# A fused GELU layer with its backward pass: two loads moved from SyncE's queue to GpSimd's, and one transposing load cut in two

## The chip, the cores and the metric

The kernel runs on one core of a Trainium2 chip. The metric is the device time of one execution in microseconds. Before the change it is 267.49 us, the median of three runs (266.95, 267.49 and 268.2). A profile adds one more execution, whose trace is what the prediction is read from.

Engines are called TensorE (PE in the profile), VectorE (DVE), ScalarE (ACT), GpSimd (POOL) and SyncE (SP). SP computes nothing here; it issues DMAs, and so do ScalarE and GpSimd.

## The reference

Everything is in bfloat16: x and grad_out are 2048 x 448, w1 is 448 x 1792, w2 is 1792 x 448. The six outputs are the layer's result and the gradients of its five inputs:

```python
def _fwd_reference(x, w1, b1, w2, b2):
    h = jnp.einsum("bsd,df->bsf", x, w1) + b1
    h = _gelu(h)                      # tanh form
    return jnp.einsum("bsf,fd->bsd", h, w2) + b2
# outputs: out, and from jax.vjp with grad_out: grad x, w1, b1, w2, b2
```

With u = x w1 + b1, q = g w2^T and gh = q * gelu'(u), the work is five big products: u, q, out = gelu(u) w2, grad x = gh w1^T, and the two weight gradients x^T gh and h^T g.

## The kernel before, in words

**Two stages.** The first, up to about 177 us, goes over the rows in 4 blocks of 512 and over the 1792 features in 7 pairs of 128-wide tiles. Each step has one pair of one block: u of a pair (transposed: features on partitions), its GELU and derivative on ScalarE and VectorE, q of a pair, gh, and shares of out and grad x. The second stage makes the weight gradients.

**Order of the first stage.** The order is written out by hand. Iteration i of the loop (i = 1 to 11) makes u of step i + 2 (tile pu, from w1_f and xT), then q of step i (pq, from w2T and gT), with products for out (ps, from hT and w2_sb) and, from iteration 6 on, for grad x (ps, from ghT and w1T_sb) between them. Nearly all of these matmuls are recorded at line 259, in half_product, which runs two half-height products side by side. The feature pairs of a block are taken in the order FP = [1, 2, 3, 4, 5, 6, 0], so tiles 0 and 1 of each weight come last. Up to step 11 there is one accumulator for q (two banks): q of step i can begin only when gh of step i - 1 has been made from it, at line 397 on VectorE.

**Where the loaded tiles are first read.** x's second block by u of step 7, in iteration 5. w2_sb's tiles 0 and 1 by out's last pair, at the end of iteration 5. b2_bc (b2 on all partitions) when the first finished out tiles are evicted by VectorE at line 437, in iteration 6. w1T_sb's tiles 2 to 7 at the end of iteration 6; its tiles 8 and 9 as the first fill of iteration 7, tiles 10 and 11 as the second, tiles 12, 13, 0 and 1 after these. g's second block by q of step 7, in iteration 7, behind the second fill.

**The loads.** All loads are issued at the top, in the order of the code on each engine's queue. SP has most of them: plain ones (load_w1, load_w2, load_rest) and transposing ones (load_x, load_g, load_w2T, and the two w1T_sb parts). Two transposing loads are never issued from different engines. GpSimd has b1 (line 143), the last rows of w1 for tiles 0 and 1 (line 175, by load_rest at line 123), held back behind one of SP's loads by behind(), and a small copy into w2T (line 176). After that GpSimd issues the stores of finished tiles of out and grad x (line 438) and a few more loads. The DMAs of SP and ScalarE use eight semaphores in turn, so that each issue waits for the landing of the one eight issues earlier; GpSimd's use eight others in the same way.

The end of SP's list, with the line numbers of the profile:

```python
    load_w2T(1280, F)                                                  # 170
    load_x(1)                                                          # 171
    load_w2(nc.sync, 0, 2)                                             # 172
    nc.sync.dma_start(out=b2_bc[:], in_=b2....to_broadcast((P, D)))    # 173
    behind(nc.gpsimd, rest)                                            # 174
    load_rest(nc.gpsimd, 0, 256)                                       # 175
    nc.gpsimd.tensor_copy(out=w2T[DL:P, 0, 0:16], in_=w2_first[...])   # 176
    load_w2T(0, 256)                                                   # 177
    nc.sync.dma_start_transpose(out=w1T_sb[:, 0:8, :], ...)            # 178
    load_g(1)                                                          # 179
    nc.sync.dma_start_transpose(out=w1T_sb[:, 8:NF, :], ...)           # 180
```

SP's next instructions are the turn of gh for the second stage (line 409, in turn_gh), further blocks of x and g, and the stores of h (line 406).

Of the kernel before, what the change touches and what calls it, by code (L numbers as in the profile page):

```python
# [19 lines left out]
def kernel(  # L20
# [15 lines left out]
    nc = tc.nc  # L36
    P = 128
    B, S, D = x.shape
    F = w1.shape[1]
    assert (B, S, D, F) == (1, 2048, 448, 1792)  # L40
    NS = S // P
    NF = F // P
# [34 lines left out]
    b2_bc = const.tile([P, D], BF16, name="b2_bc")  # L77
# [5 lines left out]
    w1T_sb = const.tile([P, NF, D], BF16, name="w1T_sb")  # L83
# [12 lines left out]
    def wide(src, r0, n, shift):  # L96
        return bass.AP(src.tensor, src.offset + r0 * D - shift, [[D, n], [1, (KF + 1) * P]])

    def load_x(b):
        t = blk.tile([P, KF + 1, SB], BF16, name="xT", tag="xT")  # L100
        r0 = ROW0[b]
        if b in WIDE:
            nc.sync.dma_start_transpose(out=t[:], in_=wide(x2, r0, SB, 0))
        else:
            nc.sync.dma_start_transpose(out=t[:, 0:KF, :], in_=x2[r0:r0 + SB, 0:KF * P])
            nc.sync.dma_start_transpose(out=t[:, KF, :], in_=x2[r0:r0 + SB, D - P:D])
        xT[b] = t

    def load_g(b):
        t = blk.tile([P, KF + 1, SB], BF16, name="gT", tag="gT")  # L110
        r0 = ROW0[b]
        if b in WIDE:
            nc.sync.dma_start_transpose(out=t[:], in_=wide(g2, r0, SB, DL))
        else:
            nc.sync.dma_start_transpose(out=t[:, 1:KF + 1, :], in_=g2[r0:r0 + SB, DL:D])
            nc.sync.dma_start_transpose(out=t[:, 0, :], in_=g2[r0:r0 + SB, 0:P])
        gT[b] = t
# [4 lines left out]
    def load_rest(eng, f0, f1):  # L122
        return eng.dma_start(out=wt1[0:DL, f0:f1], in_=w1[KF * P:D, f0:f1])

    def behind(eng, transfer):
        tc.add_manual_dep(eng.nop().ins, transfer.ins.name, mybir.DependencyInfo(mybir.DependencyClass.Sync, mybir.DependencyReason.DATA),
                          reason="loads behind what is needed first")

    def load_w2(eng, t0, t1):
        return eng.dma_start(out=w2_sb[:, t0:t1, :], in_=w2[t0 * P:t1 * P, :].rearrange("(ft p) d -> p ft d", p=P))  # L130

    def load_w2T(f0, f1):
        if f0 > 0:
            nc.sync.dma_start_transpose(out=w2T[:, :, f0:f1], in_=wide(w2, f0, f1 - f0, DL))
        else:
            nc.sync.dma_start_transpose(out=w2T[:, :, 16:f1], in_=wide(w2, 16, f1 - 16, DL))
            nc.sync.dma_start_transpose(out=w2T[:, 1:KF + 1, 0:16], in_=w2[0:16, DL:D])
# [31 lines left out]
    load_w1(nc.sync, 0, 256)  # L169
    load_w2T(1280, F)  # L170
    load_x(1)
    load_w2(nc.sync, 0, 2)
    nc.sync.dma_start(out=b2_bc[:], in_=b2.rearrange("(o d) -> o d", o=1).to_broadcast((P, D)))
    behind(nc.gpsimd, rest)
    load_rest(nc.gpsimd, 0, 256)
    nc.gpsimd.tensor_copy(out=w2T[DL:P, 0, 0:16], in_=w2_first[0:DL, :])
    load_w2T(0, 256)
    nc.sync.dma_start_transpose(out=w1T_sb[:, 0:8, :], in_=w1[:, 0:8 * P])
    load_g(1)
    nc.sync.dma_start_transpose(out=w1T_sb[:, 8:NF, :], in_=w1[:, 8 * P:F])  # L180

    pw = two_banks(1, "pw")
    for w in range(NWAKE):
# [675 lines left out]
```

## Time and profile before

| | before |
|---|---|
| median of 3 runs | 267.49 us (266.95 to 268.2) |
| profiled execution | 266.88 us |
| its span, first to last instruction | 265.1 us |
| granted TensorE clock | 1.00 of full speed throughout |
| longest share of the chain that ended last | PE, 97% |

The span is 1.78 us shorter than the execution's own time; those are what lies before the first and after the last instruction. In the profile a row of a timeline gives start, duration, engine, line, operation, what is written and what is read. SPq and POOL rows named DMA are the issuing of a transfer, not the transfer; its landing is in the DMA view, counted from the start of the issue. In the list of waits the numbers are microseconds in total, how often, and the longest.

### The profile page before, as it was taken

The numbers are of one execution on the slowest core, as the hardware profiler recorded it, in microseconds if no ns is written. First come the engines' busy times: TensorE is split into PE (matmuls) and PEld (weight loads), VectorE is DVE, ScalarE is ACT, GpSimd is POOL, SyncE is SP. The second block draws the span as 40 slices with busy tenths as digits, with TensorE's granted clock in tenths as the row PEclk, the third lists the DMA queues.
The fourth block names the chain that finished last, engine by engine and source line by source line (L and its number), as shares of the span: only waits on it lengthen the run. The fifth ranks groups of instructions, "written<-read, shape, count | busy, mean of one in ns | idle before, by whom it ended". The sixth has DMA issues, their size and how long they took to land.

```text
span 265.1 us, 5205 instructions
## 1 busy us (share of the span) xinstructions
PE 261.2 (99%) x2171; PEld 148.2 (56%) x2171; DVE 174.8 (66%) x217; ACT 137.5 (52%) x164; POOL 41.4 (16%) x52
## 2 busy tenths in 40 slices
PE   8999999999999999999999999999999999999995
PEld 3444444444466565555657887764444765555554
DVE  1699999999998978769897631129999991000000
ACT  2899997888997596877748410022111111121111
POOL 1001003300302021010311110220700008900000
PEclk9999999999999999999999999999999999999999
DMA  7999999999999999255382359999311102999851
GB/s 164 244 239 220 169 214 211 179 312 201 219 229 240 194 259 202 38 164 105 100 161 52 64 128 293 353 170 270 92 40 40 49 22 51 221 205 235 199 128 35
DMA packets 111735, 44.47 MB, mean 168 GB/s; under 512 B 91040, under 2 KB 110576, under 8 KB 111712
## 3 DMA queue, kind: packets, MB, share of 16 engines
q1 hardware_dynamic: 104608, 36.14, 64.9%
q0 software_dynamic: 1856, 4.30, 6.5%
q10 hardware_dynamic: 5248, 3.71, 4.7%
q8 instruction: 17, 0.28, 0.4%
q14 instruction: 6, 0.05, 0.1%
HBM read 7.23 MB, written 14.23 MB: 81 GB/s over the span
## 4 chain that ended last, share of the span: by engine, by line
PE 97%; DMA 2%; ACT 0%; issue 0%
PE ps L259 32%; PE ps_v L807 16%; PE pu L259 16%; PE pq L259 15%; PE ps_w L775 14%; PE ps_w L786 2%; DMA xT<-in_x_dram 2%; PE pu L238 2%; PE pu L499 0%; PE ps L425 0%; ACT st L810 0%
## 5 line engine op out<-in xcount | busy, mean ns | idle before, releaser
L259 PE MATMUL pq<-gT,w2T 64*128 64x512 bf16 x386 | 55.6, 376 | 0.0
L259 PE MATMUL ps<-w_sb,hT 64*128 64x448 bf16 x440 | 49.0, 349 | 0.0
L259 PE MATMUL ps<-w1T_sb,ghT 64*128 64x448 bf16 x448 | 48.8, 349 | 0.0
L339 ACT ACTIVATE U<-pu,b1T 128x512 bf16<-128x512 f32 x54 | 33.5, 690 | 18.6 <-PE pu L259 14.4
L807 PE MATMUL ps_v<-g_nat,h_nat 128*128 128x448 bf16 (+1 forms) x240 | 42.6, 340 | 0.0
L397 DVE SCALAR_TENSOR_TENSOR ghT<-AZ,pq 128x1024 bf16<-128x1024 bf16 x28 | 33.9, 1217 | 12.3 <-PE pq L259 11.8
L259 PE MATMUL pu<-xT,w_f 64*128 64x512 bf16 x300 | 41.4, 376 | 0.0
L438 POOL DMA_DIRECT2D out_dram<-st x32 | 19.9, 625 | 134.7 <-DVE st L437 71.8
L259 PEld LDWEIGHTS <-ghT 64*128 64x128 bf16 x448 | 28.6, 94 | 15.6
L775 PE MATMUL ps_w<-gh_nat,x_nat 128*128 128x512 bf16 (+1 forms) x192 | 36.5, 352 | 0.0
L259 PEld LDWEIGHTS <-hT 64*128 64x128 bf16 x440 | 26.4, 94 | 16.9 <-issue 0.5
L259 PEld LDWEIGHTS <-w2T 64*128 64x128 bf16 x392 | 26.3, 94 | 15.1 <-PE pq L259 0.9
L807 PEld LDWEIGHTS <-h_nat 128*128 128x128 bf16 x240 | 23.3, 98 | 19.3 <-DMA out_dram<-st 0.3
L357 ACT ACTIVATE AZ<-AZ 128x1024 bf16<-128x1024 bf16 (+1 forms) x20 | 27.8, 1392 | 6.8 <-DVE AZ L353 6.8
L761 DVE TENSOR_TENSOR acc<-acc,gh_nat 128x1792 f32<-128x1792 f32 x14 | 30.0, 2142 | 0.5
L775 PEld LDWEIGHTS <-x_nat 128*128 128x128 bf16 x192 | 18.7, 98 | 17.9 <-issue 0.4
L348 ACT ACTIVATE AZ<-U 128x1024 bf16<-128x1024 bf16 (+1 forms) x21 | 28.2, 1343 | 0.9 <-DVE U L341 0.4
L345 ACT ACTIVATE hT<-U 128x1024 bf16<-128x1024 bf16 (+1 forms) x22 | 28.0, 1278 | 0.0
L810 ACT CAST st<-ps_v 128x448 bf16<-128x448 f32 (+1 forms) x15 | 7.6, 507 | 34.8 <-PE ps_v L807 34.8
L259 PEld LDWEIGHTS <-w_f 64*128 64x128 bf16 x300 | 16.2, 94 | 14.9 <-issue 0.7
L435 ACT CAST st<-ps 128x448 bf16<-128x448 f32 x16 | 7.9, 540 | 29.4 <-PE ps L259 27.6
L778 ACT CAST st<-ps_w 128x512 bf16<-128x512 f32 (+1 forms) x12 | 6.4, 532 | 27.6 <-PE ps_w L775 24.7
(56 smaller groups left out, 189.6 us busy)
## 6 DMA issues: line engine op xcount, KB each, us to landing
hT_dram<-hT SPq DMA_DIRECT2D x28, 256.0 KB, 3.3
out_dram<-st POOLq DMA_DIRECT2D x32, 112.0 KB, 4.8
x_nat<-in_x_dram SPq DMA_DIRECT2D x1, 1792.0 KB, 10.3
g_nat<-in_grad_out_dram SPq DMA_DIRECT2D x1, 1792.0 KB, 15.6
out_dram<-st ACTq DMA_DIRECT2D x13, 112.0 KB, 3.3
out_dram<-st ACTq DMA_DIRECT2D x9, 128.0 KB, 1.7
w_f<-in_w_dram SPq DMA_DIRECT2D x5, 192.0 KB, 4.0
w_sb<-in_w_dram SPq DMA_DIRECT2D x4, 224.0 KB, 3.9
```

What stands on the lines that cost most here:

```text
L259: mm = nc.tensor.matmul(ps, lhsT=w, rhs=m, start=start, stop=stop, tile_position=(hf.start, 0), skip_group_check=True)
L339: nc.scalar.activation(out=dst, in_=PU[f][a][:], func=ACT.Identity, bias=bias)
L345: nc.scalar.activation(out=rows(hT, r), in_=part_u(r), func=ACT.Gelu_apprx_tanh)
L348: nc.scalar.activation(out=part_a(ks), in_=part_u(ks), func=ACT.Square, scale=math.sqrt(3.0 * GELU_A * GELU_C))
L357: nc.scalar.activation(out=z, in_=z, func=ACT.Tanh, scale=-1.0 / 3.0)
L397: nc.vector.scalar_tensor_tensor(out=rows(ghT, [k]), in0=part_z([k]), scalar=1.0, in1=PQ[k][:], op0=ALU.subtract if single else ALU.add, o ...
L435: nc.scalar.copy(out=st[:, 0:D], in_=self.ps)
L438: pooled.append(nc.gpsimd.dma_start(out=(out2 if self.kind == "o" else gx2)[r:r + P, :], in_=st[:, 0:D]))
L761: last_sum[:] = [nc.vector.tensor_tensor(out=v, in0=in0, in1=gh_nat[:, b, :, j, :], op=ALU.add)]
L775: nc.tensor.matmul(ps[:, 0:n * P], lhsT=x_nat[:, st_, kt * P:(kt + 1) * P], rhs=gh_nat[:, b, ft0:ft0 + n, j, :], start=(st_ == 0), stop=(s ...
L807: nc.tensor.matmul(ps[:, 0:w], lhsT=h_nat[ft][:, st_, :], rhs=g_nat[:, st_, h * w:(h + 1) * w], start=(st_ == 0), stop=(st_ == NS - 1))
L810: done = nc.scalar.copy(out=o[:, 0:w], in_=ps[:, 0:w])
```

## The change

Two loads that SP issued, w2's tiles 0 and 1 and the broadcast of b2, are issued by GpSimd, behind its load of w1's last rows and its small copy. The load of w1T_sb's tiles 8 to 13, which SP issued behind g's second block, is cut into two: tiles 8 and 9 ahead of g's second block, tiles 10 to 13 behind it. Nothing is computed differently, and the same bytes are loaded.

```diff
     load_x(1)
-    load_w2(nc.sync, 0, 2)
-    nc.sync.dma_start(out=b2_bc[:], in_=b2.rearrange("(o d) -> o d", o=1).to_broadcast((P, D)))
     behind(nc.gpsimd, rest)
     load_rest(nc.gpsimd, 0, 256)
     nc.gpsimd.tensor_copy(out=w2T[DL:P, 0, 0:16], in_=w2_first[0:DL, :])
+    load_w2(nc.gpsimd, 0, 2)
+    nc.gpsimd.dma_start(out=b2_bc[:], in_=b2.rearrange("(o d) -> o d", o=1).to_broadcast((P, D)))
     load_w2T(0, 256)
-    nc.sync.dma_start_transpose(out=w1T_sb[:, 0:8, :], in_=w1[:, 0:8 * P])
+    def load_w1T(t0, t1):
+        nc.sync.dma_start_transpose(out=w1T_sb[:, t0:t1, :], in_=w1[:, t0 * P:t1 * P])
+
+    load_w1T(0, 8)
+    load_w1T(8, 10)
     load_g(1)
-    nc.sync.dma_start_transpose(out=w1T_sb[:, 8:NF, :], in_=w1[:, 8 * P:F])
+    load_w1T(10, NF)
```

The order of the matmuls, and of VectorE's and ScalarE's instructions, is the same in both kernels. TensorE's first read of w1T_sb's tiles 10 and 11 waits for the third part, which is a wait more than before. On GpSimd the two issues come ahead of all line-438 stores.

## The prediction

> **What bounds the kernel now.** I read the page first, then the list of waits of TensorE, then the timelines of TensorE and of SP's queue around the moved loads. The page has the busy times and the chain that ended last:
>
> ```profile
> span 265.1 us, 5205 instructions
> PE 261.2 (99%) x2171; PEld 148.2 (56%) x2171; DVE 174.8 (66%) x217; ACT 137.5 (52%) x164; POOL 41.4 (16%) x52
> PE 97%; DMA 2%; ACT 0%; issue 0%
> ```
>
> The list of waits of TensorE, complete:
>
> ```profile
> PE pw L184 <- PEq L843: 0.8, 1, 0.8
> PE pu L238 <- DMA xT<-in_x_dram: 0.2, 1, 0.2
> ```
>
> TensorE is busy for 261.2 of 265.1 us and waits twice, for 1.0 us in all, both times in the first 6 us, before anything the change touches. After that it never waits in this execution. So no load in the middle of the kernel can give this execution time back; a moved load can only take time, or take away a wait that this execution happens not to have. What matters is therefore the slack of each load: when it landed, and when it is first used. SP's queue, as issued (start, duration):
>
> ```profile
> 24.04 3.00 SPq L103 DMA_TRANSPOSE xT<-in_x_dram  x1
> 27.08 0.58 SPq L130 DMA_DIRECT2D w_sb<-in_w_dram  x1
> 27.70 0.47 SPq L173 DMA_DIRECT2D b_bc<-in_b_dram  x1
> 28.21 1.22 SPq L136 DMA_TRANSPOSE w2T<-in_w_dram  x1
> 29.48 1.22 SPq L137 DMA_TRANSPOSE w2T<-in_w_dram  x1
> 30.75 4.39 SPq L178 DMA_TRANSPOSE w1T_sb<-in_w_dram  x1
> 35.18 2.49 SPq L113 DMA_TRANSPOSE gT<-in_grad_out_dram  x1
> 37.72 3.39 SPq L180 DMA_TRANSPOSE w1T_sb<-in_w_dram  x1
> 41.22 3.79 SPq L409 DMA_TRANSPOSE gh_nat<-ghT  x1
> ```
>
> SP goes back to back here, some 0.05 us between two issues, so each issue's duration pushes the next. The time from an issue's start to its landing, from the DMA view of each issue's own short window, for the xT, w_sb, first w1T, gT and second w1T rows above, in this order:
>
> ```profile
> xT<-in_x_dram SPq DMA_TRANSPOSE x1, 5.0
> w_sb<-in_w_dram SPq DMA_DIRECT2D x1, 224.0 KB, 2.9
> w1T_sb<-in_w_dram SPq DMA_TRANSPOSE x1, 7.4
> gT<-in_grad_out_dram SPq DMA_TRANSPOSE x1, 5.2
> w1T_sb<-in_w_dram SPq DMA_TRANSPOSE x1, 5.5
> ```
>
> And the first uses on TensorE (and, for b2, on VectorE):
>
> ```profile
> 33.01 0.81 PE L259 MATMUL pu<-xT,w_f 64*128 64x512 bf16 x6
> 37.17 0.54 PE L259 MATMUL ps<-w_sb,hT 64*128 64x448 bf16 x4
> 39.47 1.15 DVE L437 TENSOR_TENSOR st<-ps,b_bc 128x448 bf16<-128x448 f32 x2
> 43.48 0.54 PE L259 MATMUL ps<-w1T_sb,ghT 64*128 64x448 bf16 x4
> 43.86 0.81 PE L259 MATMUL pu<-xT,w_f 64*128 64x512 bf16 x6
> 44.51 0.54 PE L259 MATMUL ps<-w1T_sb,ghT 64*128 64x448 bf16 x4
> 44.89 0.38 PE L259 MATMUL pq<-gT,w2T 64*128 64x512 bf16 x1
> ```
>
> By the code the row at 33.01 opens iteration 5 and is the first to read x's second block; 37.17 is the seventh feature pair (FP[6] = 0), so w2's tiles 0 and 1; 43.48 in iteration 7 reads w1T tiles 8 and 9, 44.51 tiles 10 and 11, and 44.89 is the first use of g's second block. The second w1T part landed at 37.72 + 5.5 = 43.22 and was needed at 43.48: **0.26 us of slack**, by far the least. g's block: 35.18 + 5.2 = 40.38 for 44.89, 4.5 us. x's block: 29.04 for 33.01, 4.0 us. w2's tiles: 29.98 for 37.17, 7.2 us.
>
> **The change part by part.** *SP loses two issues.* From 27.08 to 28.21 SP issued w2's two tiles and b2; without them everything behind starts 1.13 us earlier. The two w2T pieces and the first w1T part take 28.21 to 35.18, 6.97 us, so they now run from 27.08 to 34.05.
>
> *The split.* The six-tile issue (3.39) becomes a two-tile and a four-tile issue. No row shows either size of w1T. The nearest small ones:
>
> ```profile
> 0.72 1.34 SPq L146 DMA_TRANSPOSE xT<-in_x_dram  x1
> 2.12 1.31 SPq L149 DMA_TRANSPOSE xT<-in_x_dram  x1
> ```
>
> Each moves 256 rows by 512 columns; two w1T tiles are 448 rows by 256, slightly less data, so I take 1.3 (bounds: 1.13, a third of 3.39, and 2.49, g's whole block). For four tiles: two thirds of 3.39 is 2.26, half of the eight-tile 4.39 is 2.20; I take 2.3 (bounds 2.2 and 3.39). So tiles 8 and 9 go out at 34.05, g's block at 34.05 + 1.3 + 0.05 = 35.40 (0.22 later than now), tiles 10 to 13 at 35.40 + 2.49 + 0.05 = 37.94, over at 40.24. At the upper bounds, 2.49 and 3.39, g starts at 36.59 and the last part ends at 42.52.
>
> *What that does to the slacks.* The second part now lands 43.22 - 41.11 = 2.1 us after its issue ends, the first one 38.15 - 35.14 = 3.0. Tiles 8 and 9 then land at 35.35 + 3.0 = 38.4 for 43.48: slack 5.1. g lands at 35.40 + 5.2 = 40.6 for 44.89: 4.3 (3.1 at the upper bound). Tiles 10 to 13 land at 40.24 + 2.1 = 42.3 for 44.51: 2.2. At both upper bounds that is 44.6, a wait of 0.1. So the least slack of this stretch goes from 0.26 to about 2.2 us. TensorE gets one more wait, for the third w1T part; behind it stand all later matmuls, but it should be over before TensorE arrives. Behind the split SP turns gh (41.22 now, about 40.3 then), whose results are read only in the last third.
>
> *POOL gets two issues.* They come behind POOL's load of w1's last rows and its copy:
>
> ```profile
> 23.05 0.61 POOL L123 DMA_DIRECT2D wt<-in_w_dram  x1 [21.11 <-DMA w_f<-in_w_dram]
> 23.72 0.38 POOL L176 COPY w2T<-w_first 64x16 bf16<-64x16 bf16 x1
> 40.38 1.49 POOL L438 DMA_DIRECT2D out_dram<-st  x2 [16.28 <-DVE st L437]
> DMA to landing us min/median/max: 2.0/4.8/9.2
> q0 software_dynamic: 1856, 4.30, 6.5%
> ```
>
> (The fourth line is the landing of all L438 stores from POOL, the fifth is POOL's queue on the page.) w2's issue starts at 24.10, b2's behind it. One L438 store (128 rows) costs 1.49 / 2 = 0.75 us of POOL, the 64-row load 0.61; w2 has 256 row pieces, so between 0.61 and an estimated 1.5. POOL is then free by 26.4 at the latest and has nothing to do until 40.38. By the slowest L438 landing, 9.2 us, w2's tiles are there at 33.3 (use at 37.17) and b2 by 34.8 (use at 39.47). Both covered; that costs nothing.
>
> *The same bytes, three microseconds sooner.* 336 KB now run beside the transposes in flight from 24 us. POOL's queue spent 0.065 x 265.1 = 17.2 us of 16 engines on 4.30 MB, 4.0 us a MB, so these 0.34 MB take 1.4 us. If all of it falls on x's second block, that lands at 30.4 instead of 29.04, for 33.01. Covered.
>
> [...] VectorE beside POOL's issue, and the matmul that waits for VectorE:
>
> ```profile
> 22.15 0.69 DVE L387 TENSOR_SCALAR AZ<-AZ 128x2048 bf16<-128x2048 bf16 x1 [0.27 <-ACT AZ L357]
> 23.36 0.69 DVE L391 TENSOR_TENSOR AZ<-AZ 128x1024 bf16<-128x1024 bf16 x1
> 24.30 1.21 DVE L397 SCALAR_TENSOR_TENSOR ghT<-AZ,pq 128x1024 bf16<-128x1024 bf16 x1
> 40.53 0.68 DVE L387 TENSOR_SCALAR AZ<-AZ 128x2048 bf16<-128x2048 bf16 x1
> 25.81 0.38 PE L259 MATMUL pq<-gT,w2T 64*128 64x512 bf16 x1
> 22.50:25.00 2.50, 2.50 (x28) 1.20 (x26) 2.50 (x5) 2.47 (x4) 1.00 (x2) 1.00 1.23 287
> 25.00:27.50 2.50, 2.50 (x28) 1.18 (x26) 2.50 (x5) 2.32 (x4) 0.00 (x0) 1.00 1.06 183
> ```
>
> (The last two are stretches of time, with the busy time of TensorE, weight loads, VectorE, ScalarE and POOL after the comma.) VectorE took 0.69 for L391 while POOL issued at 23.05 to 23.66, and 0.68 for L387 beside POOL's two stores at 40.38, as against 0.69 at 22.15 with POOL idle: neither engine seems to hold up the other. [...]
>
> **Sum.** For an execution like the profiled one: 0, thus 266.88 (span 265.1 and 1.78 around it). The median of the three runs shown is 267.49, they reach from 266.95 to 268.2, so the usual run is 0.6 above the profiled one. The one place after the start where a run could lose that is the 0.26 us of slack at 43.48: a load that lands 0.9 us later there costs 0.6. If that is where it is lost, the change takes it back. I put most of the 0.6 there: **267.0**.
>
> **The rivals.** *It does nothing:* the 0.6 us lie in start, end or clocks, which no row can tell from a single execution; then 267.5. For it: the profiled run itself did not wait. Against it: issues of one size differ by more than that (x's block 3.00, g's 2.49), and 0.26 is little.
>
> *The runs of before wait longer than these three:* a wait of 1.3 us at 43.48, as the 268.2 run could have had, would be the rule where both are measured; then the change is worth over 0.5%, at some 266.2 to 266.9 as the base goes.
>
> *Slower, POOL holds up VectorE:* the two issues fall at 24.1 to 26.4. From 22.5 to 27.5 VectorE is busy for 2.50 of each 2.50 us, and gh of pair 2 (24.30 + 1.21 = 25.51) frees the only accumulator for the matmul at 25.81: 0.30 us of slack. If VectorE stands still while POOL issues, it loses at most 1.5 + 0.75 = 2.25 us; 0.30 are covered, 1.95 go on the path, and TensorE has no gap in which to make them up: 266.88 + 1.95 = 268.8, or 269.4 from the median. It decides from 0.30 us of hold-up on. Against it stand the equal VectorE rows above.
>
> *Slower, w2 comes too late:* it has 37.17 - 24.10 = 13.1 us. Only a landing beyond that, 1.4 times the slowest L438 store, matters; at twice the slowest, 18.4, TensorE waits 5.3 us: 272.2.
>
> **How the numbers follow.** About 0.5% (1.34 us; bounds 266.15 and 268.83) is what a measurement of this kernel can tell from no change. Forecast (the 0.26 us go, 266.5 to 267.4) 0.50; nothing 0.34; longer waits before 0.06; POOL against VectorE 0.07, of which 0.06 beyond the bound; w2 late 0.03. Hence faster 0.06, same 0.85, slower 0.09. Forecast and nothing, each with some 0.4 either way for the scatter of a median, reach from 266.4 to 267.9; to take in some of the slower case, and the waits of 0.1 at the split's upper bounds, I go to 268.3.
>
> **What would show it.** After: SP's two w2T pieces start about 1.1 us earlier behind x's block; a two-tile issue of 1.1 to 1.5 us ahead of g; the four-tile one over near 40.2, landing near 42.3. TensorE's list of waits keeps its two lines at the start and no other. POOL's two new issues start near 24.1, and VectorE's rows at 24 to 28 keep their durations. A third line in TensorE's list (w_sb near 37, w1T_sb or gT near 44, pq near 26) would prove the sum wrong, and so would a median under 266.15, since no wait of that size is in the trace.

## The result, and the profile after

| | before | after |
|---|---|---|
| median | 268.31 us (22 runs) | 266.92 us (22 runs) |
| lowest to highest | 266.63 to 271.46 | 266.55 to 272.13 |
| profiled execution, its span | 266.88, 265.1 us | 266.8, 265.0 us |
| ratio after to before | | 0.9964, 95% interval 0.9946 to 0.9981 |

The ratio leaves out the runs more than 1.5% above the fastest of their kernel; the traces below show that in this kernel such a run can be the work of the very wait that the change aims at, so the medians of all runs (1.4 us apart) say more here. The two profiled executions differ by 0.1 us: both are good ones. What changed is how many runs are good. In this comparison 15 of before's 22 runs are above 267.75 us, which is 0.9 us above the median of a kernel without the wait (c1 below), and 2 of after's 22. Over all comparisons of this study, before was above 267.75 us in 113 of 162 runs (with b1 and c2 below counted as before), after in 3 of 34; the lowest runs are the same (266.43 and 266.48).

TensorE's list of waits in the trace after, complete:

```profile
PE pw L188 <- PEq L847: 0.8, 1, 0.8
PE pu L242 <- DMA xT<-in_x_dram: 0.2, 1, 0.2
```

No third line, as before. SP's queue (start, duration; the two w1T issues at 29.20 are merged, a narrower window shows the first alone):

```profile
23.57 2.98 SPq L103 DMA_TRANSPOSE xT<-in_x_dram  x1
26.59 1.30 SPq L136 DMA_TRANSPOSE w2T<-in_w_dram  x1
27.93 1.22 SPq L137 DMA_TRANSPOSE w2T<-in_w_dram  x1
29.20 6.38 SPq L179 DMA_TRANSPOSE w1T_sb<-in_w_dram  x2
29.20 5.05 SPq L179 DMA_TRANSPOSE w1T_sb<-in_w_dram  x1
35.63 2.21 SPq L113 DMA_TRANSPOSE gT<-in_grad_out_dram  x1
37.88 2.00 SPq L179 DMA_TRANSPOSE w1T_sb<-in_w_dram  x1
40.00 2.80 SPq L413 DMA_TRANSPOSE gh_nat<-ghT  x1
```

The w2T pieces follow x's block directly, and the last w1T issue is over at 39.88, where the second part ended at 41.11 before. Landings from the start of the issue: tiles 8 and 9 (their window's summary), g's block, tiles 10 to 13, then w2's two tiles and b2 on POOL's queue, and x's second block on SP's:

```profile
DMA to landing us min/median/max: 3.7/3.7/3.7
gT<-in_grad_out_dram SPq DMA_TRANSPOSE x1, 4.9
w1T_sb<-in_w_dram SPq DMA_TRANSPOSE x1, 4.4
w_sb<-in_w_dram POOLq DMA_DIRECT2D x1, 224.0 KB, 6.5
b_bc<-in_b_dram POOLq DMA_DIRECT2D x1, 112.0 KB, 6.3
xT<-in_x_dram SPq DMA_TRANSPOSE x1, 7.7
```

The first uses on TensorE are where they were:

```profile
43.44 0.54 PE L263 MATMUL ps<-w1T_sb,ghT 64*128 64x448 bf16 x4
44.47 0.54 PE L263 MATMUL ps<-w1T_sb,ghT 64*128 64x448 bf16 x4
44.85 0.38 PE L263 MATMUL pq<-gT,w2T 64*128 64x512 bf16 x1
```

Tiles 8 and 9 landed at 34.30 + 3.7 = 38.0 for 43.44 (5.4 us of slack), g at 40.53 for 44.85 (4.3), tiles 10 to 13 at 42.28 for 44.47 (2.2). Before, the least slack was 0.26. x's second block now landed at 23.57 + 7.7 = 31.27, where it landed at 29.04 before; u of step 7 reads it at 32.97.

### The profile page after: what moved, and what is told of

Its sections match the earlier page's. It is cut to its first block, busy times and chain, and to the rows that moved or that the text cites. A ratio compares the mean times of both kernels' runs of the same rounds, so it can differ in the third digit from the quotient of the medians.

```text
span 265.0 us, 5207 instructions
## 1 busy us (share of the span) xinstructions
PE 261.2 (99%) x2171; PEld 148.2 (56%) x2171; DVE 174.8 (66%) x217; ACT 137.4 (52%) x164; POOL 43.0 (16%) x54
## 2 busy tenths in 40 slices
DMA packets 111479, 44.47 MB, mean 168 GB/s; under 512 B 91072, under 2 KB 110240, under 8 KB 111456
## 4 chain that ended last, share of the span: by engine, by line
PE 97%; DMA 2%; ACT 0%; issue 0%
PE ps L263 32%; PE ps_v L811 16%; PE pu L263 16%; PE pq L263 15%; PE ps_w L779 14%; PE ps_w L790 2%; DMA xT<-in_x_dram 2%; PE pu L242 2%; PE pu L503 0%; PE ps L429 0%; ACT st L814 0%
```

## The experiments

Theory: before's surplus is TensorE's wait for the second w1T part in iteration 7. Rivals: it lies at the start, in clocks, or at another load. All kernels ran beside runs of before on the same chip, 12 runs each:

| kernel | median, all runs | above 267.75 | ratio, interval |
|---|---|---|---|
| b1 before again | 267.98 | 6 | 0.9961, 0.9933 to 0.9990 |
| b2 move only | 267.74 | 6 | 0.9945, 0.9913 to 0.9976 |
| b3 split only | 267.21 | 2 | 0.9968, 0.9945 to 0.9991 |
| b4 one more load ahead | 270.03 | 11 | 1.0036, 1.0000 to 1.0073 |
| c1 nobody reads the part | 266.83 | 0 | 0.9951, 0.9925 to 0.9977 |
| c2 stores reordered | 267.86 | 7 | 1.0011, 0.9977 to 1.0045 |
| c3 after again | 266.91 | 1 | 0.9958, 0.9931 to 0.9986 |
| c4 move only again | 267.47 | 3 | 0.9975, 0.9945 to 1.0005 |
| d1 stores truly later | 268.44 | 11 | 0.9997, 0.9961 to 1.0034 |
| d2 part ahead of g | 267.71 | 6 | 0.9952, 0.9915 to 0.9989 |
| d3 move, part ahead of g | 267.07 | 1 | 0.9956, 0.9920 to 0.9993 |
| e1 four tiles, g, two | 266.81 | 1 | 0.9963, 0.9933 to 0.9993 |

Read the ratios with b1 in mind: the unchanged kernel came out at 0.9961 against itself, with an interval that leaves out 1. Before's runs are so uneven that twelve of them do not repeat to better than 0.4%, and by the ratio alone after (0.9964) cannot be told from before. So I go by traces and by how many runs are late.

**b1, before again.** No edit.

> The kernel before, unchanged, for another trace of it. Theory (the wait is at the second w1T part, 0.26 us of slack): about two runs in three are above 267.3, and then the list of waits of TensorE has a line ps L259 behind the DMA of w1T_sb near 43.5 us, of 0.5 to 2.5 us, which is the whole of the run's surplus over 266.7. Rival (time lost at the start, or by clocks): a run above 267.3 shows no such line, but a longer wait for xT or w1 in the first 10 us, or a clock under 1.00. Ratio 0.999 to 1.001 either way.

Its trace (268.21 us, span 266.4) has the third line in TensorE's list of waits, and the late matmul in the timeline:

```profile
PE ps L259 <- DMA w1T_sb<-in_w_dram: 1.2, 1, 1.2
37.18 3.59 SPq L180 DMA_TRANSPOSE w1T_sb<-in_w_dram  x1
w1T_sb<-in_w_dram SPq DMA_TRANSPOSE x1, 7.6
44.86 0.56 PE L259 MATMUL ps<-w1T_sb,ghT 64*128 64x448 bf16 x4 [1.19 <-DMA w1T_sb<-in_w_dram]
```

The part was issued earlier than in the first trace (37.18, not 37.72) and landed later, at 44.78 instead of 43.22: 4.0 us after the end of its issue instead of 2.1. The wait of 1.19 is nearly all of the 1.3 us by which the span is longer. TensorE also waited 1.0 us for x at the start, but its first real matmul began at 5.80, against 5.77 in the first trace: that wait only makes up for the eleven matmuls into pw ahead of it, which took 4.07 us instead of 4.85. The expected ratio near 1 is the miss named above.

**b4, the part issued later.**

```diff
     load_g(1)
+    idle = const.tile([P, 16], BF16, name="idle")
+    nc.sync.dma_start_transpose(out=idle[:], in_=w2[0:16, 0:P])
     nc.sync.dma_start_transpose(out=w1T_sb[:, 8:NF, :], in_=w1[:, 8 * P:F])
```

> Before, with one more small transposing load (16 rows into an unused tile, about 1.2 us of SyncE's queue) between g's block and the second w1T part. Nothing is left out. Theory: slack 0.26 - 1.25 = -1.0 us, so every run waits; the profile has a wait of TensorE at line 259 for w1T_sb near 43.5 of 1.0 us or more, and the median is 1.0 to 1.3 us above that of before (ratio 1.004 to 1.005). Rival (that load is not on the path): 0.999 to 1.001 and no such line.

The extra issue took 1.22 us; the trace has this wait and nothing new elsewhere:

```profile
PE ps L261 <- DMA w1T_sb<-in_w_dram: 2.5, 1, 2.5
```

Eleven of twelve runs are above 269, half above 270.4. The load is on the path, and its price was underestimated (see the clock below). Not every run waited as expected: one, at 266.63, cannot have lost much there.

**c1, nobody reads the part.**

```diff
-    w[hf, 2 * FP[t // 2] + t % 2, :]
+    w[hf, (2 * FP[t // 2] + t % 2) % (NF if un.kind == "o" else 8), :]
```

(The same index in Unit.emit.) This kernel leaves something out: grad x is made from eight of the fourteen tiles of w1T_sb, so its values are not those of the layer. The number and the shapes of the matmuls stay the same.

> Before, with every load in its place, but grad x is made from w1T tiles 0 to 7 alone (tile index modulo 8), so that nobody reads the second w1T part: grad x is not computed, and only the wait is gone. Theory (the whole surplus of before is the wait at the second part): like the kernel after, median 266.7 to 267.1, no undisturbed run above 267.75, no third line in TensorE's list of waits; ratio 0.995 to 0.9975. Rival (part of the surplus lies elsewhere): median 267.5 or more, with the spread of before.

Twelve runs from 266.51 to 267.18, none above. TensorE's list of waits, complete:

```profile
PE pw L184 <- PEq L843: 0.8, 1, 0.8
PE pu L238 <- DMA xT<-in_x_dram: 0.7, 1, 0.7
PE pq L259 <- DMA w2T<-in_w_dram: 0.3, 1, 0.3
```

The third line, which I had not expected, is a wait at 12.2 us, far ahead of w1T_sb. With the loads, the queues and the amount of arithmetic in place and only the wait for w1T_sb gone, before's whole spread is gone. The rivals of start and clock fall. It is also the floor: after's 266.9 is within 0.1 us of it.

**b2 and c4, the move alone.** The diff's first half.

> w2's two tiles and b2 issued by GpSimd, the second w1T part left whole. Theory: the part is issued 1.1 us sooner, slack 0.26 + 1.13 = 1.4 us instead of 0.26; ratio 0.9965 to 0.998 to before, median 266.9 to 267.5, a few runs still late. Rival (the second part is not where time is lost): ratio 0.999 to 1.001. Rival (POOL holds up VectorE): 1.002 or more.

> The move to GpSimd alone, once more: its first twelve runs had five above 267.75 although its one trace had no wait, and the trace had 1.0 us of slack at 43.4. Theory (landing varies by about 2 us, so 1.0 to 1.4 us of slack cover only part): a third to a half of the undisturbed runs above 267.4, and a traced run above 267.4 has a wait for w1T_sb of 0.3 to 1.5 us near 43.4. Rival (the move costs time somewhere else): such a run has its wait at another tile, w_sb near 37 or pq near 26.

24 runs, 9 above 267.75; b2's median, 267.74, is later than the expected 267.5. c4's trace has a 2.0 us wait for w1T_sb and none at w_sb or pq; b2's trace has none of the three. So the move helps only partly. In c4 the part was issued at 37.91, no sooner than in before, because the first w1T part ahead of it took 6.65 us to issue instead of 4.39. The same trace shows a price of the move, at x's second block: its landing, and its first use on TensorE.

```profile
29.07 6.65 SPq L178 DMA_TRANSPOSE w1T_sb<-in_w_dram  x1
xT<-in_x_dram SPq DMA_TRANSPOSE x1, 9.4
32.77 0.82 PE L259 MATMUL pu<-xT,w_f 64*128 64x512 bf16 x6
```

x's block was issued at 23.29 and landed at 32.69, 0.1 us before its use. In the six traces with the two loads on GpSimd's queue it took 7.0 to 9.4 us to land, in the eight without 4.8 to 5.1.

**b3, the split alone.** The diff's second half.

> The second w1T part cut in two with two tiles ahead of g's block, w2 and b2 left on SyncE. Theory: tiles 10 to 13 land near 43.5 for 44.5, slack 1.0 us, tiles 8 and 9 have some 4 us, g's block some 3 us; ratio 0.997 to 0.9985, so part of the gain but less than by the move alone. Rival (the second part is not where time is lost): 0.999 to 1.001.

Two of 12 runs above 267.75; I had expected the move to give more than the split. Its trace, of the 268.68 us run, has a wait of 1.7 us, now at the third part, which landed 5.0 us after the end of its issue (39.79 + 6.5 against 41.34). Which half gives more, these runs don't settle, and 2 in 12 cannot be told from the 3 in 34 of both halves together.

**c2 and d1, are the stores in the way?** GpSimd's first two stores start at 40.4 us, while the part is in flight. c2 only issued them behind the third and fourth tiles' evictions in the code:

> Before, with the first two stores of finished out tiles held back by GpSimd, from about 40.4 us to about 45.6 us, behind the next two tiles. Nothing is left out. The second w1T part landed 2.1 us after the end of its issue in the first trace and 4.0 us in the second, with these stores under way in both. Theory A (the stores in flight hold up its landing): it lands about 2.1 us after its issue in every run, the waits at 43.5 are gone or under 0.3 us, median 266.8 to 267.2. Theory B (the landing varies for another reason): the spread of before stays, about half of the undisturbed runs above 267.75, and a traced run over 267.5 shows the wait for w1T_sb.

The edit changes only GpSimd's own order and makes it wait for nothing new, so they still left at 40.40: c2 is another before, and is counted as one above. Its trace has a wait of 2.8 us for w1T_sb. d1 makes GpSimd wait for the third tile:

```diff
-            pooled.append(nc.gpsimd.dma_start(out=..., in_=st[:, 0:D]))
+            waiting.append((..., st))
+            if holding[0]:                          # holding = [2]
+                holding[0] -= 1
+            else:
+                if len(waiting) > 1:
+                    behind(nc.gpsimd, made[-1])     # the third tile's VectorE addition
+                for dst, tile_ in waiting:
+                    pooled.append(nc.gpsimd.dma_start(out=dst, in_=tile_[:, 0:D]))
+                waiting.clear()
```

> Before, with GpSimd made to wait for the third finished out tile before it issues the first store, so that the first two stores leave at about 45.4 us instead of 40.4 us (the run that only reordered GpSimd's list left them at 40.4). Nothing is left out. Theory A (the stores in flight hold up the landing of the second w1T part): it lands about 2.1 us after the end of its issue, TensorE waits under 0.3 us at 43.5, median 266.8 to 267.2. Theory B (the landing varies for another reason): the spread of before, median 267.6 to 268.6, and a traced run over 267.5 has the wait for w1T_sb.

POOL's stores, then the second part, its landing, and TensorE's wait:

```profile
46.21 2.23 POOL L445 DMA_DIRECT2D out_dram<-st  x4 [21.55 <-DVE st L437]
38.26 3.68 SPq L180 DMA_TRANSPOSE w1T_sb<-in_w_dram  x1
w1T_sb<-in_w_dram SPq DMA_TRANSPOSE x1, 7.2
PE ps L259 <- DMA w1T_sb<-in_w_dram: 1.7, 1, 1.7
```

With no store before 46.21 the part still landed 3.5 us after its issue ended (45.46 against 41.94). Theory A falls; none of d1's runs is under 267.67. Why the landing varies stays open: from 2.1 to 4.2 us after the end of the issue for the whole part (eight traces), from 2.4 to 5.0 for tiles 10 to 13 (three). SP's turn of gh, which follows right behind the part in every trace, was not taken away.

**d2 and d3, the whole part ahead of g's block.** load_g(1) behind the second part; d3 with the move as well.

> Before, with the second w1T part, whole, ahead of g's second block; w2 and b2 stay on SyncE. Theory: w1T's part then has some 2.5 us more (issued at 35.2 instead of 37.7), g's block starts at about 38.6 and lands at 43.8 to 45.8 for 44.9, so the wait moves to g: a traced slow run has a wait of pq for gT near 44.9 of up to 1 us and none for w1T_sb; ratio 0.995 to 0.999. Rival (only w1T matters): as the kernel after, no wait, 0.995 to 0.997.

> The move to GpSimd, and the second w1T part whole ahead of g's block: one issue fewer than the kernel after. Theory: g's block starts at about 37.5 and lands at 42.5 to 44.5 for 44.9, w1T's part lands by 42; at least 0.4 us for both, so no wait at all: median 266.7 to 267.0, no undisturbed run above 267.75, level with the kernel after (266.9) and with the one without a reader (266.83). Rival (g's landing varies as much as w1T's): some runs wait for gT near 44.9, median 267.1 or more.

The wait moves to g, in both. TensorE's line in d2, g's issue and landing there, and TensorE's line in d3:

```profile
PE pq L259 <- DVE AZ L387: 1.2, 1, 1.2
39.48 2.51 SPq L113 DMA_TRANSPOSE gT<-in_grad_out_dram  x1
gT<-in_grad_out_dram SPq DMA_TRANSPOSE x1, 7.1
```

```profile
PE pq L259 <- DMA gT<-in_grad_out_dram: 0.4, 1, 0.4
```

d2's line is a lesson in reading: it names VectorE's L387, which q does not depend on (in the first trace q began at 44.89, ahead of the same L387 row at 45.81). g landed at 39.48 + 7.1 = 46.58, and q's matmul began at 46.58. d3 has the same wait with its right name. So g's block may not be pushed back by a whole w1T part; a smaller piece fits ahead of it, two tiles in after, four in e1 below, where g landed at 36.43 + 5.8 = 42.23 for 45.01.

**e1, four tiles ahead of g, two behind.**

```diff
-    load_w1T(8, 10)
+    load_w1T(8, 12)
     load_g(1)
-    load_w1T(10, NF)
+    load_w1T(12, NF)
```

> The kernel after, with four tiles of the second w1T part ahead of g's block and two behind it, instead of two and four. The last two tiles are first read at 45.3 instead of 44.5, so the last landing has some 0.8 us more, and g's block, issued about 1 us later, still has about 3 us. Theory (after's runs of 267.2 and above are the rest of the same wait): no undisturbed run above 267.4, median 266.7 to 266.9, level with the kernel in which nobody reads the part (266.83). Rival (that rest lies elsewhere): the spread of after, about three in ten above 267.2; or g is late and the wait moves to pq near 44.9.

One run of 12 above 267.2 (268.09, where none above 267.4 was expected); after has 10 of 34. That is too little to call, and so is 266.81 against 266.92. In its trace the last two tiles landed at 39.86 + 4.8 = 44.66 for 45.44, so the slack there is 0.8 us, not more than after's 2.2. No trace shows where 268.09 came from.

## Why the prediction was right or wrong

**Right: the bound, and the profiled execution.** TensorE had nothing to gain in that trace, and the trace after is 0.1 us from it.

**Right: the split.** Tiles 8 and 9 took 6.38 - 5.05 - 0.05 = 1.28 us to issue (1.3 predicted), the other four 2.00 (2.3), and they landed at 42.28 (42.3). The slacks came out at 5.4, 4.3 and 2.2 (5.1, 4.3 and 2.2). That they fit so closely is in part luck, as the next point shows.

**Wrong: what the move gives SP.** The step "everything behind starts 1.13 us earlier" takes each issue to last as long as before. In after the first w1T part took 5.05 us to issue instead of 4.39; from the start of x's issue to the end of this part's it took 10.68 us instead of 11.10, a gain of 0.4. The forecast times were met because x's issue began 0.47 us earlier in this trace (23.57, not 24.04), ahead of anything that the change touches, and because g's block and the last four tiles took 0.3 us less each. Over the traces that stretch took 10.2 to 12.4 us with the move (six, mean 10.9) and 10.5 to 11.5 without (eight, mean 10.9). The 1.13 us are not seen.

**Wrong: what the move costs x.** The prediction let x's second block land at most 1.4 us later. It landed 2 to 4.4 us later after its issue, and of its 4.0 us of slack after's trace kept 1.7 and c4's 0.1. TensorE did not wait for it in a way that a list of waits shows, but this was nearer than "covered".

**Right: VectorE is not held up, and w2 is in time.** POOL's rows after, and VectorE's beside them:

```profile
24.00 0.77 POOL L130 DMA_DIRECT2D w_sb<-in_w_dram  x1
24.77 0.57 POOL L176 DMA_DIRECT2D b_bc<-in_b_dram  x1
23.31 0.69 DVE L395 TENSOR_TENSOR AZ<-AZ 128x1024 bf16<-128x1024 bf16 x1
24.25 1.21 DVE L401 SCALAR_TENSOR_TENSOR ghT<-AZ,pq 128x1024 bf16<-128x1024 bf16 x1
25.38 0.68 DVE L388 TENSOR_TENSOR AZ<-AZ,hT 128x1024 bf16<-128x1024 bf16 x1
```

1.34 us in all, under the bound of 2.25, with every VectorE row as long as before, and w2's tiles there at 30.5 for 37.1. Both slower rivals fall. The two issues took 0.77 and 0.57 us beside a busy VectorE, where SP's took 0.58 and 0.47 before. The landings were longer than from SP's queue, though (6.5 and 6.3 us against 2.9 and 3.9), and no run here shows why, or whether they and x's block slowed each other.

**Right: the place.** The 0.26 us at 43.5 were where runs were lost; b1, b4 and c1 show it from three sides. I had only argued it from the smallness of the slack.

**Wrong: the size.** The step that failed is "the usual run is 0.6 above the profiled one", read from three runs. Over 162 runs before's median is 268.47, 1.6 above the 266.83 of c1, so what the change takes back is 1.4 us by the medians, not the forecast 0.5. The predicted 267.0 held because it started from the floor. The rival "the runs of before wait longer than these three" had 0.06; it was nearer the truth than my forecast's size, though the ratio stays within 0.5%.

**Wrong: one landing taken for all.** I gave the part 2.1 us from the end of its issue to its landing. The whole part takes 2.1 to 4.2. Its issue also ends at different times, from 40.8 to 42.3 us in the five traces that leave SP's list as it was. Together they turned 0.26 us of slack into waits of 1.2 us (b1) to 2.8 us (c2, whose issue ended 1.1 us later than in the first trace). After's 2.2 us are not quite safe either: in c3's trace the third part landed at 38.56 + 5.8 = 44.36 and TensorE began it at 44.43 instead of 44.19. One of c3's twelve runs, at 269.14, has no trace.

## What to carry to other kernels

A single trace without a wait does not prove that there is none: look for the load with the least slack between landing and first use, and hold that slack against how much landings of its kind vary (here 2.1 to 4.2 us after the end of the issue), not against one landing. When a kernel's runs are uneven, a trace of a bad run is worth more than a better average; then take away only the suspected wait (other data, same traffic) and see whether the spread goes with it. To buy slack, issue what is needed first in pieces of the size of its first use: with two tiles ahead of g's block, and the move, the least slack was 2.2 us instead of 0.26. Moving plain loads to another engine's queue can have a price that must be looked for: here the transposing load beside them landed 2 to 4.4 us later.

## What the hardware did that I had not expected

The longer waits cost more than themselves. After a wait of 2.0 us TensorE's clock was granted at half for over 3 us. In c4's trace, by stretches of 2 us (TensorE's busy time after the comma, the granted clock third from last), and then in d1's, whose wait was 1.66 us:

```profile
44.00:46.00 2.00, 0.62 (x6) 0.37 (x7) 2.00 (x5) 0.05 (x1) 0.60 (x1) 0.91 0.56 127
46.00:48.00 2.00, 2.00 (x14) 0.89 (x11) 1.77 (x4) 0.00 (x0) 2.00 (x5) 0.50 0.83 149
48.00:50.00 2.00, 2.00 (x18) 0.94 (x16) 0.00 (x0) 1.03 (x2) 0.46 (x1) 0.73 1.25 340
```

```profile
44.00:46.00 2.00, 0.46 (x6) 0.30 (x7) 2.00 (x5) 0.52 (x1) 0.00 (x0) 1.00 0.73 119
46.00:48.00 2.00, 2.00 (x24) 1.09 (x22) 2.00 (x5) 0.43 (x1) 1.79 (x4) 1.00 0.97 154
```

The clock lost in c4's three stretches is 2 x (0.09 + 0.50 + 0.27) = 1.7 us; with the wait of 1.97 that makes 3.7, just what its span of 268.7 has over 265.0. The traces with waits of 2.5 us (b4) and 2.8 us (c2) show 0.50 as well and lose the same 1.7 us of clock; those with 1.2 (b1), 1.66 (d1) and 1.7 us (b3) stay at 1.00. That fits the runs of before from 270.4 us up: every one whose clock is on record has a mean clock of 0.987 to 0.994, and it would explain the half of b4's runs above 270.4. In these six traces the longest wait with no such fall behind it was 1.7 us (b3), the shortest with one 1.97 us (c4). Two of after's 34 runs are at 271.8 and 272.1 with a mean clock of 0.993 and 0.994; no trace of such a run was taken, so that they too waited is only likely.
